# One of seven block products, P4, moved behind the last unit and taken in two levels

## The chip, the cores and the metric

The kernel runs on one core of a Trainium2 chip. Its time is device microseconds of that core, the median of a few runs. The engines are PE (TensorE: matmuls, with PEld its weight loads), DVE (VectorE), ACT (ScalarE), POOL (GpSimd, used here mostly to issue transfers) and SP (SyncE, which issues the loads of q, k and v).

## The reference

Everything is float32 here. A linear attention with decay is followed by a two-layer block:

```python
for b in range(nb):                       # blocks of 64 tokens
    intra = ((qb @ kb.T) * Dmask) @ vb    # Dmask = lam ** (i - j) below the diagonal
    inter = (qb * lam_pow) @ kv_state
    out = intra + inter
    kv_state = lam ** 64 * kv_state + (kb * rev_pow).T @ vb
x = out as (3072 tokens, 512)
h = x @ w_in                              # (512, 2048): the first product
g = h - tanh(h)
return g @ w_out                          # (2048, 512): the second product
```

## The kernel before, in words

The 3072 tokens go through in six groups (`NG`, g = 0 to 5) of 512 tokens: 128 positions of each of four sequences. Each group has an attention part, a first product and a second product; the attention of group g + 1 is woven into the products of group g.

**Strassen's seven products.** The 2048 columns of `w_in` are cut into four units u of 512. Within a unit weights and tokens are two by two blocks, and the product is taken as the Winograd form of Strassen's method: seven products P1 to P7 of half-sized blocks instead of eight. `FACT` (line 596) names the two factors of each; P4 is A22 (the second half of the unit's columns, the second half of the 512 inner rows) times T4 (a combination of tokens). The four results of a unit are `hidden(g, 11)`, `12`, `21` and `22` (in the trace all `g`), each 128 partitions by 512 columns per unit. P4 counts in 21 alone.

**Two levels.** In groups from the third on (`GI = 2`), P1 and P5 are cut once more: `inner_steps` (line 728) takes each as seven products of quarter blocks, each step for all four units at once, 4 matmuls of 128 columns. Its small weight combinations come from DRAM (`fine_in`), where `inner_weights` (line 706) writes them once, during the second group; its token combinations are made by `inner_tokens` (line 716). P2, P3, P4, P6 and P7 are one level: `up` (line 626) issues 4 matmuls of 256 columns for one unit. The second product is in two levels too: `down_twice` (line 915), seven steps of 4 matmuls of 128 columns.

**One unit** (`up`, lines 632 to 675). P1 and P5 have been added up in SBUF (`gS` and result 22). ACT seeds three PSUM banks from there (`seeded`, line 618): w, y and z. P2 adds to w, P6 and then P7 and P4 to y, P3 to z. Out of w comes 11; the state of y after P6 is copied into 12 (line 661), to which z is added (line 673); the state after P7 is added to 22 (line 664); y after P4 is 21. Each result r becomes r - tanh(r): tanh on ACT into a `th` tile (line 650, two buffers), the subtraction on DVE (line 655). Then two sums follow on DVE (`up_sums`, lines 697 and 698).

**The order.** `later_units` (line 1238) writes the order out. Unit 0: P2 of the next unit, P3, sums, P4. Units 1 and 2: P6, P2 of the next unit, P7, P3, sums, P4. Unit 3: P6, P3, P7, sums, the quarter sums for the second product's first part (`sums_twice(g, 4)`, three DVE operations of 512 columns), then the "cover", then P4. The cover is an attention block of the next group (`att_both`: lines 510, 496, 460, 524, ending in two copies by ACT into `xt`, line 414); in the sixth group it is product 1 of the second product (`down`, line 869). Then `later_products` starts with `down_twice(g, 4)`.

**What sets order and waits.** Operations marked `tied` or `hold` stay in program order on their engine; the others are placed by the tile framework's scheduler. Each engine runs its queue in order. Of the eight PSUM banks four are `ya`, `yb`, `w` and `z`, and four rotate under the tag `att`: the attention block takes two for its results and two for scores, and the two accumulators of `down_twice(g, 4)` take the next in turn, which are those two of the results that the xt copies read. The pieces of the second product's weights are loaded by POOL into a ring of 7 tiles, in the order of `pieces_of` (line 772): a load is issued when a tile of the ring comes free. Small sums of tokens, weights and quarters share one pool of four tiles (`sums`). In the third group DVE and POOL also make the fine weight combinations for two more parts (`fine_factors`, line 843: `made[g, 1]` and `made[g, 2]`, four adds each, given out along the units).

Of the kernel before, what the change touches and what calls it, by code (L numbers as in the profile page):

```python
# [24 lines left out]
def kernel(  # L25
# [116 lines left out]
    def tied(yes, op):  # L142
        return tc.keep_in_program_order(op) if yes else op
# [74 lines left out]

    fine_in = dram.tile([2, 3, 128, NU, 128], F32, name="fine_in")
    w_in_u = moe_w_in.rearrange("k (u a n) -> k u a n", u=NU, a=2)  # L220
# [405 lines left out]
    def up(g, u, n, wait=False, inside=False):  # L626
# [30 lines left out]
        if g >= GI:  # L657
            if n == 2:
                finish(11, t)
            elif n == 6:  # L660
                nc.scalar.activation(dst(12), t, AF.Copy)
            elif n == 7:
                def end():
                    tied(inside, nc.vector.tensor_tensor(dst(22), dst(22), t, op=AL.add))  # L664
                    finish(22, dst(22))

                if wait:
                    return end
                end()
            elif n == 4:  # L670
                finish(21, t)
            else:
                tied(inside, nc.vector.tensor_tensor(dst(12), dst(12), t, op=AL.add))  # L673
                finish(12, dst(12))
            return
# [23 lines left out]

    INNER = (1, 5)  # L700
    toks = {}

    def a_quarter(n, u, i, k):
        return w1[u][:, k, 0, ts(i, 128)] if n == 1 else ws[u][:, 0, k, ts(i, 128)]

# [9 lines left out]

    def inner_tokens(g):
        for n in INNER:
            x = xt[g][FACT[n][1]]
# [3 lines left out]
            for dst, x, y in ((t1, b12, b11), (t2, b22, t1), (b12, b22, b12), (t4, b21, t2)):  # L722
                nc.vector.tensor_tensor(dst, x, y, op=AL.subtract)
            toks[g, n] = {1: b11, 2: b21, 3: b22, 4: t4, 5: t1, 6: t2, 7: b12}

    STEPS = (1, 5, 2, 6, 7, 3, 4)

    def inner_steps(g, n, tag):
# [4 lines left out]
        for x in STEPS:  # L733
            b = toks[g, n][x]
            wb = piece(g, ("in", n), x) if x in (3, 5, 6) else None
            dst = w if x == 2 else z if x in (3, 5) else y
            for u in range(NU):
                a = wb.rearrange("p m c -> p (m c)")[:, ts(u, 128)] if wb is not None else a_quarter(
                    n, u, *{1: (0, 0), 2: (0, 1), 7: (1, 0), 4: (1, 1)}[x])
                tied(True, nc.tensor.matmul(out=dst[:, ts(u, 128)], lhsT=a, rhs=b, start=x in (1, 2, 5) and u == 0,  # L740
                                            stop=True, skip_group_check=True))
            d = dst.rearrange("q (u c) -> q u c", u=NU)
# [29 lines left out]
    def pieces_of(g):  # L772
        if g >= GI:
            yield from ((g, ("in", 5), x) for x in STEPS if x in (5, 6, 3))
        for n in order(g):
# [462 lines left out]
    def later_units(g):  # L1238
        for n in (1, 2):
            made[g, n] = fine_factors(n) if g == GI else iter(())  # L1240
        for u in range(NU):
            if u < 2:
                next(made[g, u + 1], None)
            for n in ("next", 3, "S", 4) if u == 0 else (6, "next", 7, 3, "S", 4) if u + 1 < NU else (
                    6, 3, 7, "S", "P4", "cover", 4):
                if n == "next":
                    up(g, u + 1, 2, inside=True)
                elif n == "S":
                    up_sums(g, u)
                elif n == "P4":  # L1250
                    sums_twice(g, 4)
                elif n == "cover":
                    if twice(g, 1):
# [6 lines left out]
            if u == 0:  # L1260
                every(made[g, 1])
            elif u == NU - 1:
                every(made[g, 2])

# [37 lines left out]
    for g in range(1, NG):  # L1302
# [6 lines left out]
        if g == NG - 1:  # L1309
            down_end(g)  # L1310
            continue
        inner_tokens(g + 1)
        p3 = down_twice(g, 3)
# [47 lines left out]
```

## Time and profile before

| | us |
|---|---|
| median of three runs (656.47 to 660.67) | 657.89 |
| the profiled execution | 657.6 |
| its span, first to last instruction | 655.8 |
| PE busy | 642.0 |
| DVE busy | 494.0 |
| ACT busy | 241.3 |
| POOL busy | 230.9 |
| mean granted PE clock | 0.997 of full speed |

A line of the timeline gives the start, the duration, the engine, the line of the kernel, the operation, the tile written and the tiles read, the shape and the count; in brackets the idle time of the engine before it and what ended it. One float32 matmul shows as two MATMUL records, so a step of 4 matmuls is "x8". The displayed duration of matmuls contains the end of the pipeline; the time that a step takes is from its start to the start of the next. A line of a stage gives the stretch, its length, the busy time of PE, PEld, DVE, ACT and POOL with the number of instructions, the granted clock, and the DMA engines' share and rate.

### The profile page before, as it was taken

To read this page: it belongs to the slowest core of one execution; us is meant where nothing else is said; L and a number is where in the kernel's file an instruction comes from. 1 tells how busy PE (TensorE), PEld (TensorE's weight loads), DVE (VectorE), ACT (ScalarE), POOL (GpSimd) and SP (SyncE) were. 2 spreads that over 40 slices of the span, in tenths; PEclk is the share of its full clock that TensorE was granted. 3 is DMA by queue.
4 is the path that set the end of the run, shared out by engine and by line. 5 is a ranking of instruction groups with operands and counts; after the bars stand their busy time and mean duration, and the time that the engine had idled before them with its cause. 6 is when DMAs were issued, how large, how long until landed. Compare 5 with 4: busy or idle time off the path is not lost.

```text
span 655.8 us, 14778 instructions
## 1 busy us (share of the span) xinstructions
PE 642.0 (98%) x5792; PEld 590.4 (90%) x5792; DVE 494.0 (75%) x884; ACT 241.3 (37%) x484; POOL 230.9 (35%) x396
## 2 busy tenths in 40 slices
PE   8899899999999999999999999999999999999998
PEld 6688688888888999989999988999988999988997
DVE  4688788896975986898868787878777888356583
ACT  3688565422321223443122453222354212444110
POOL 2120145775012545342556100546301356300450
PEclk9999999999999999999999999999999999999999
DMA  9979958999558877999878776779692487610582
GB/s 215 216 208 186 246 182 271 338 324 329 133 138 202 265 240 256 229 258 283 302 245 286 198 143 141 230 238 298 204 198 97 149 293 254 212 43 0 157 280 79
DMA packets 108261, 140.45 MB, mean 214 GB/s; under 512 B 64032, under 2 KB 81568, under 8 KB 108192
## 3 DMA queue, kind: packets, MB, share of 16 engines
q0 software_dynamic: 29840, 97.54, 46.5%
q1 hardware_dynamic: 78208, 41.96, 27.7%
q8 instruction: 46, 0.75, 0.5%
q14 instruction: 23, 0.19, 0.1%
q10 hardware_dynamic: 144, 0.00, 0.0%
HBM read 117.18 MB, written 23.86 MB: 215 GB/s over the span
## 4 chain that ended last, share of the span: by engine, by line
PE 75%; DVE 4%; DMA 3%; issue 1%; POOL 1%; ACT 1%; DVEq 0%; ACTq 0%; POOLq 0%
PE y L642 17%; PE y L934 16%; PE zw L934 12%; PE z L642 6%; PE w L642 5%; PE y L740 4%; PE z L740 2%; PE acc L1044 2%; PE y L869 2%; DMA wb<-fine 2%; PE sp L460 2%; PE op L510 1%; PE op L496 1%; PE w L740 1%; PE end L993 1%
## 5 line engine op out<-in xcount | busy, mean ns | idle before, releaser
L816 POOL DMA_DIRECT2D wb<-fine x217 | 116.7, 539 | 216.8 <-PE y L934 110.3
L934 PE MATMUL y<-wb,g 128*128 128x128 f32 x624 | 81.3, 276 | 0.5 <-DVE ss L467 0.4
L937 ACT ACTIVATE q<-y 128x128 f32<-128x128 f32 x108 | 29.9, 277 | 135.0 <-PE y L934 135.0
L934 PEld LDWEIGHTS y<-wb,g 128*128 128x128 f32 x624 | 75.3, 192 | 1.3 <-DVE ss L467 0.5
L934 PE MATMUL zw<-wb,g 128*128 128x128 f32 x416 | 55.2, 276 | 0.7 <-DMA wb<-fine 0.7
L934 PEld LDWEIGHTS zw<-wb,g 128*128 128x128 f32 x416 | 50.6, 192 | 1.1 <-DMA wb<-fine 1.1
L1014 PE MATMUL h<-xt,w 128*128 128x256 f32 x192 | 45.9, 393 | 1.1 <-DVE w L325 1.1
L642 PE MATMUL y<-xt,w 128*128 128x256 f32 x200 | 46.9, 380 | 0.0
L650 ACT ACTIVATE th<-g 128x512 f32<-128x512 f32 x42 | 26.5, 630 | 51.8 <-DVE g L673 19.7
L1014 PEld LDWEIGHTS h<-xt,w 128*128 128x128 f32 x192 | 36.8, 196 | 7.1 <-DVE w L325 1.0
L642 PEld LDWEIGHTS y<-xt,w 128*128 128x128 f32 x200 | 37.6, 190 | 5.1 <-ACT g L682 0.2
L655 DVE TENSOR_TENSOR g<-g,th 128x512 f32<-128x512 f32 x42 | 29.1, 692 | 17.4 <-ACT th L650 17.2
L642 PE MATMUL w<-xt,w 128*128 128x256 f32 x168 | 40.4, 382 | 0.0
L642 PE MATMUL z<-xt,ws 128*128 128x256 f32 x168 | 39.7, 379 | 0.0
L642 PE MATMUL y<-tt,w 128*128 128x256 f32 x160 | 38.1, 381 | 0.0
L642 PE MATMUL y<-tt,ws 128*128 128x256 f32 x160 | 38.1, 380 | 0.0
L642 PEld LDWEIGHTS z<-xt,ws 128*128 128x128 f32 x168 | 31.9, 190 | 4.3
L642 PEld LDWEIGHTS w<-xt,w 128*128 128x128 f32 x168 | 31.0, 190 | 4.5 <-ACT w L613 0.4
L642 PEld LDWEIGHTS y<-tt,w 128*128 128x128 f32 x160 | 30.1, 190 | 4.3 <-DVE g L664 0.2
L642 PEld LDWEIGHTS y<-tt,ws 128*128 128x128 f32 x160 | 30.0, 190 | 3.9
L934 PE MATMUL y<-wb,s 128*128 128x128 f32 x248 | 32.8, 275 | 0.1
L934 PE MATMUL zw<-wb,s 128*128 128x128 f32 x248 | 32.8, 275 | 0.0
(216 smaller groups left out, 1373.6 us busy)
## 6 DMA issues: line engine op xcount, KB each, us to landing
wb<-fine POOLq DMA_DIRECT2D x217, 256.0 KB, 3.8
fine<-f POOLq DMA_DIRECT2D x24, 256.0 KB, 5.3
wb<-fine_in POOLq DMA_DIRECT2D x24, 256.0 KB, 4.2
raw<-in_moe_w_out_dram POOLq DMA_DIRECT2D x10, 512.0 KB, 6.6
raw<-in_moe_w_in_dram SPq DMA_DIRECT2D x8, 512.0 KB, 5.2
raw<-in_moe_w_in_dram SPq DMA_DIRECT2D x16, 256.0 KB, 6.3
q_blk<-in_q_dram SPq DMA_DIRECT2D x32, 128.0 KB, 3.9
k_blk<-in_k_dram SPq DMA_DIRECT2D x32, 128.0 KB, 4.7
```

The costliest lines, as they stand in the source:

```text
L460: tied(True, nc.tensor.matmul(out=dst, lhsT=keys(p, j, late_), rhs=qt[ts(j, 64), p, rows], start=True, stop=True))
L496: tied(True, nc.tensor.matmul(out=dst(n, pp, j), lhsT=state[r, b, pp, :], rhs=tr[g, b][2][r, pp, :], start=not begun and n == 0 and p == 0 ...
L642: tied(g == 0, nc.tensor.matmul(out=t[:, m, :], lhsT=wt[:, kt, ts(m, 128)], rhs=x[:, kt, :], start=first and m == 0 and kt == 0, stop=kt = ...
L650: tied(g == 0, nc.scalar.activation(th, src, AF.Tanh))
L655: tied(g == 0 or g >= GI and inside, nc.vector.tensor_tensor(dst(c), src, th, op=AL.subtract))
L740: tied(True, nc.tensor.matmul(out=dst[:, ts(u, 128)], lhsT=a, rhs=b, start=x in (1, 2, 5) and u == 0, stop=True, skip_group_check=True))
L816: nc.gpsimd.dma_start(out=t.rearrange("p m c -> p (m c)"), in_=fine[TWICE.index(n_), SLOT.index(x_)].rearrange("p u c -> p (u c)"))
L869: nc.tensor.matmul(out=t[:, m, :], lhsT=a[:, u, kt, ts(m, 128)], rhs=wb[:, kt, :], start=first and u == 0 and m == 0 and kt == 0, stop=u = ...
L934: tied(True, nc.tensor.matmul(out=dst, lhsT=a[:, u, :], rhs=wb[:, ts(u, 128)], start=x in begins and u == 0, stop=u == NU - 1, skip_group_ ...
L937: nc.scalar.activation(keep, dst, AF.Copy)
L1014: tied(u == 0 or u == 2 and cs[0] == 11, nc.tensor.matmul(out=hm[c][:, m, :], lhsT=w1[u][:, i, a, ts(m, 128)], rhs=xt[0, t][:, i, :], star ...
L1044: nc.tensor.matmul(out=acc[n][:, r, :], lhsT=a[:, ts(r, 128)], rhs=b, start=kt == 0 and r == 0, stop=kt == KH - 1, skip_group_check=True)
```

## The change

From the third group on, P4 of the four units is no longer taken unit by unit. After P7 of each unit ACT copies the state of y into result 21. Behind unit 3's sums one new step, `inner_last`, takes P4 of all four units in two levels: seven sub-steps of 4 matmuls of 128 columns, in the banks ya, w, z and one of `att`. ACT copies three of its intermediate states, DVE adds four of them to the quarters of result 21. Behind the three quarter sums for the second product, `finish_last` adds the last intermediate state (one DVE operation of 1024 columns) and does the four tanh and the four subtractions of result 21. The cover then has no P4 behind it.

The small weight combinations of A22 are written during the second group beside those of P1 and P5 (4 DVE operations and one transfer more a unit); three more pieces a group are loaded through the ring. The token combinations of T4 are made by four small DVE operations: in the third group behind unit 3's sums and the last of the factor adds, later ahead of unit 3's P6. The last factor add moves from behind the last unit to behind unit 3's sums.

On ACT's queue the changed program has, at the end of the first product of the third to fifth group: the copy w, tanh of 22, the copy r5, the copy z, the probe of the attention block, the four tanh of result 21, the two xt copies. In the sixth group the four tanh stand before the copy of product 1.

```diff
-    INNER = (1, 5)
+    INNER = (1, 5, 4)
     def a_quarter(n, u, i, k):
-        return w1[u][:, k, 0, ts(i, 128)] if n == 1 else ws[u][:, 0, k, ts(i, 128)]
+        return (w1[u][:, k, 0] if n == 1 else ws[u][:, 0, k] if n == 5 else w1[u][:, 2 + k, 1])[:, ts(i, 128)]
...
             elif n == 7:
                 def end():
+                    nc.scalar.activation(dst(21), t, AF.Copy)
                     tied(inside, nc.vector.tensor_tensor(dst(22), dst(22), t, op=AL.add))
...
+    def inner_matmuls(g, n, x, dst, begin):
+        b = toks[g, n][x]
+        wb = piece(g, ("in", n), x) if x in (3, 5, 6) else None
+        for u in range(NU):
+            a = wb.rearrange("p m c -> p (m c)")[:, ts(u, 128)] if wb is not None else a_quarter(
+                n, u, *{1: (0, 0), 2: (0, 1), 7: (1, 0), 4: (1, 1)}[x])
+            tied(True, nc.tensor.matmul(out=dst[:, ts(u, 128)], lhsT=a, rhs=b, start=begin and u == 0,
+                                        stop=True, skip_group_check=True))
+
+    LAST = (1, 5, 6, 2, 7, 3, 4)
+
+    def inner_last(g):
+        y, w, z5, z3 = bank("y3", "ya", 1), bank("w3", "w", 1), bank("z5", "att", 4), bank("z3", "z", 1)
+        r5 = otile("r5")
+        out4 = hidden(g, 21)
+        c11, c12, c21, c22 = (out4[:, :, i, ts(j, 128)] for i in range(2) for j in range(2))
+        for x in LAST:
+            dst = {2: w, 3: z3, 5: z5}.get(x, y)
+            inner_matmuls(g, 4, x, dst, x in (1, 5))
+            if x in (1, 6):
+                nc.scalar.activation(w if x == 1 else z3, y, AF.Copy)
+            elif x == 5:
+                nc.scalar.activation(r5, z5, AF.Copy)
+            else:
+                c = {2: c11, 7: c22, 3: c12, 4: c21}[x]
+                hold(c, c, dst.rearrange("q (u c) -> q u c", u=NU), op=AL.add)
+        return r5
+
+    def finish_last(g, r5):
+        c = hidden(g, 21)
+        cols = c[:, :, :, ts(1, 128)]
+        hold(cols, cols, r5.rearrange("q (u c) -> q u c", u=NU)[:, :, None, :].to_broadcast([128, NU, 2, 128]), op=AL.add)
+        for u in range(NU):
+            th = work.tile([128, 2, HB], F32, name="th", tag="th")
+            nc.scalar.activation(th, c[:, u], AF.Tanh)
+            hold(c[:, u], c[:, u], th, op=AL.subtract)
...
-            yield from ((g, ("in", 5), x) for x in STEPS if x in (5, 6, 3))
+            yield from ((g, ("in", n), x) for n in (5, 4) for x in STEPS if x in (5, 6, 3))
...
-            for n in ("next", 3, "S", 4) if u == 0 else (6, "next", 7, 3, "S", 4) if u + 1 < NU else (
-                    6, 3, 7, "S", "P4", "cover", 4):
+            for n in ("next", 3, "S") if u == 0 else (6, "next", 7, 3, "S") if u + 1 < NU else (
+                    ("T",) * (g > GI) + (6, 3, 7, "S") + ("T",) * (g == GI) + ("U4", "P4", "cover")):
...
                 elif n == "S":
                     up_sums(g, u)
+                    if u + 1 == NU:
+                        every(made[g, 2])
+                elif n == "T":
+                    inner_tokens(g, (4,))
+                elif n == "U4":
+                    r5 = inner_last(g)
                 elif n == "P4":
                     sums_twice(g, 4)
+                    finish_last(g, r5)
...
             if u == 0:
                 every(made[g, 1])
-            elif u == NU - 1:
-                every(made[g, 2])
```

More of the change, by code (lines that the diff above doesn't have):

```diff
@@ L217 @@
     fine = dram.tile([len(TWICE), len(SUB), 128, NU, 128], F32, name="fine")
-    fine_in = dram.tile([2, 3, 128, NU, 128], F32, name="fine_in")
+    fine_in = dram.tile([3, 3, 128, NU, 128], F32, name="fine_in")
     w_in_u = moe_w_in.rearrange("k (u a n) -> k u a n", u=NU, a=2)
@@ L714, in inner_weights, with inner_tokens @@
             nc.gpsimd.dma_start(out=fine_in[INNER.index(n)].rearrange("x p u c -> p u x c")[:, u], in_=t[:, 0:3])
-    def inner_tokens(g):
-        for n in INNER:
+    def inner_tokens(g, ns):
+        for n in ns:
             x = xt[g][FACT[n][1]]
@@ L722, in inner_tokens @@
             for dst, x, y in ((t1, b12, b11), (t2, b22, t1), (b12, b22, b12), (t4, b21, t2)):
[L723 removed]
+                tied(n == 4, nc.vector.tensor_tensor(dst, x, y, op=AL.subtract))
             toks[g, n] = {1: b11, 2: b21, 3: b22, 4: t4, 5: t1, 6: t2, 7: b12}
     STEPS = (1, 5, 2, 6, 7, 3, 4)
+    def inner_matmuls(g, n, x, dst, begin):
[31 more added lines that the diff above has]
+            hold(c[:, u], c[:, u], th, op=AL.subtract)
     def inner_steps(g, n, tag):
@@ L733, in inner_steps @@
         for x in STEPS:
-            b = toks[g, n][x]
-            wb = piece(g, ("in", n), x) if x in (3, 5, 6) else None
             dst = w if x == 2 else z if x in (3, 5) else y
[L737 to L741, printed above, removed]
+            inner_matmuls(g, n, x, dst, x in (1, 2, 5))
             d = dst.rearrange("q (u c) -> q u c", u=NU)
@@ L1311 @@
             continue
-        inner_tokens(g + 1)
+        inner_tokens(g + 1, (1, 5))
         p3 = down_twice(g, 3)
```

## The prediction

> **What bounds the kernel now.** I read the page's totals first, then what the matmul engine (PE) waited for, then busy time by stage, then the timeline around the edited place in the fourth group (g = 3).
>
> ```profile
> PE 642.0 (98%) x5792; PEld 590.4 (90%) x5792; DVE 494.0 (75%) x884; ACT 241.3 (37%) x484; POOL 230.9 (35%) x396
> ```
>
> ```profile
> PE zw L934 <- DMA wb<-fine: 0.7, 2, 0.3
> PE sp L460 <- DVE kt L354: 0.5, 2, 0.3
> PE y L934 <- DVE ss L467: 0.4, 1, 0.4
> ```
>
> ```profile
> 272.00:307.00 35.00, 35.00 (x332) 30.88 (x333) 31.28 (x48) 15.66 (x29) 9.11 (x15) 1.00 1.09 275
> 376.00:411.00 35.00, 35.00 (x329) 31.00 (x326) 26.77 (x40) 15.71 (x29) 0.00 (x0) 1.00 0.69 140
> ```
>
> PE is the bound: 98% busy, and these three, its only listed waits from the second group on, come to 1.6 us in all (waited-for line, total, times, longest). The two stage rows (third and fourth group, first product; after the span the columns are PE, PEld, DVE, ACT, POOL) say more: PE is full, but DVE is at 31.3 and 26.8 of 35 us, so it has little room. Whatever shortens PE there meets DVE next.
>
> ```profile
> 395.77 1.89 PE L642 MATMUL z<-xt,ws 128*128 128x256 f32 x8
> ...
> 397.49 1.89 PE L642 MATMUL y<-tt,w 128*128 128x256 f32 x8
> ...
> 398.13 0.70 DVE L673 TENSOR_TENSOR g<-g,z 128x512 f32<-128x512 f32 x1
> ...
> 398.93 0.63 ACT L650 ACTIVATE th<-g 128x512 f32<-128x512 f32 x1 [1.55 <-DVE g L673]
> ...
> 399.22 1.89 PE L642 MATMUL y<-tt,ws 128*128 128x256 f32 x8
> 399.46 0.58 ACT L618 ACTIVATE z<-g 128x512 f32<-128x512 f32 x1
> ...
> 400.95 1.89 PE L642 MATMUL z<-xt,ws 128*128 128x256 f32 x8
> ...
> 404.49 1.15 PE L510 MATMUL op<-ss,v_nat 128*64 128x64 f32 x32
> ...
> 407.84 0.70 PE L524 MATMUL op<-ss,v_nat 64*64 64x64 f32 x32
> ...
> 408.46 1.99 PE L642 MATMUL y<-tt,w 128*128 128x256 f32 x8
> 408.52 1.08 ACT L414 ACTIVATE xt<-op 128x512 f32<-128x512 f32 x2 [1.60 <-PE op L524]
> ...
> 410.30 1.05 PE L934 MATMUL y<-wb,g 128*128 128x128 f32 x8
> 410.56 0.60 ACT L650 ACTIVATE th<-y 128x512 f32<-128x512 f32 x1 [0.95 <-PE y L642]
> ...
> 411.19 1.06 PE L934 MATMUL zw<-wb,g 128*128 128x128 f32 x8
> ```
>
> In order: P3 of unit 2, its P4, P6 and P3 of unit 3. P3 of unit 3 waits for the seed of bank z (399.46 to 400.04), which stands behind unit 2's add and tanh; P4 at 397.49 is part of what hides that. Below: the attention block (404.49 to 408.46), then P4 of unit 3, which hides the two copies xt (408.52 to 409.60) before the second product begins at 410.30. That product's two accumulators lie in the banks those copies empty. So P4 is cover at both places.
>
> **The change, part by part.**
> PE. A P4 step (4 matmuls of 256 columns) is 1.727 us from start to start (395.77 to 397.49); four make 6.91 a group. The new form is 7 steps of 4 matmuls of 128 columns, each 0.893 (410.30 to 411.19): 6.25. Gain 0.66 a group, 2.6 over four groups, if nothing waits.
>
> Second group: 16 more small DVE subtractions (0.28 long, 0.20 apart, 0.8 a unit) and 4 more writes of fine_in. DVE idles 0.7 to 1.2 in each unit's chain there, which covers 0.8. POOL gets one write ahead of the second product's pieces, 0.76 of issuing; the last piece is needed about 6 us later. Without that cover: up to 1. I take 0.
>
> Loads: three more pieces a group (256 KB, 4.2 us to landing) in the ring of 7; while they sit there, four of the next product's pieces are fetched early instead of seven. Each new piece still has about 6.2 us before use, and the waits below add to that. 0; bounds 0 and 0.35 a group (the longest such wait in the trace).
>
> Fourth group, walked on the trace's clock.
> (a) Unit loop: without three P4 steps P3 of unit 3 could start at 400.95 - 5.18 = 395.77. The z seed ends 4.27 after P3 of unit 2 starts (400.04 - 395.77); that part of DVE's order is unchanged. P3 of unit 3 now comes two steps (3.45) later instead of three, so it waits 4.27 + 0.1 - 3.45 = 0.9. The other seeds (w, y) and the copies out of y, one more on ACT per unit, come out 0.05 to 0.2 ahead of PE. P3 starts at 396.65, P7 at 398.4, the new step at 400.1.
> (b) The new step: DVE still owes the last unit's two adds, two subtractions and two sums when it begins, and is free for the new adds (0.68 each, as the P5 adds of L892) at 404.4. PE's last sub-step must wait for the second of its four adds to leave bank y: 0.35. The step ends at 406.7.
> (c) The attention block follows, 0.1 + 3.97, to 410.75; nothing of P4 is left behind it.
> (d) ACT's queue in the changed program holds the four new tanh ahead of the two xt copies. Each tanh waits for DVE: the last add (from 406.85, 0.6), three sums for the second product (0.7, 0.6, 0.6), then one add of 1024 columns (1.22, as L838), to 410.57. Then tanh 0.63, and, as the th tile has two buffers, the third and fourth wait for the first and second subtraction: starts 410.6, 411.15, 412.0, 412.7. The first xt copy runs 413.25 to 413.85, and the second product starts at 413.95. It started at 410.30: 3.65 lost, of which 3.2 is this wait.
> Queued behind it: on PE the whole second product; on DVE, after the fourth subtraction, that product's next sums, of which the first is due 1.8 after its start, when DVE has been free since 414.0. The end of (d) is the new bound: eight links of DVE and ACT, 7.2 us, against 4.07 of attention block. Bounds for one group: -0.66 (all hidden), +4.6 (every margin of 0.05 to 0.2 missed).
>
> The fifth group has the same order and work: 3.65.
>
> Third group: DVE also makes the fine factors (8 adds L892, 0.7 each). Four stand in one run from 280.9 to 283.8, as before, and DVE is then the bound: following its order at the trace's spacing (0.6 between independent instructions, 0.72 between dependent ones, 0.95 for a transpose, one subtraction of P4 taken out), the z seed of unit 3 ends at 294.75 (before 296.67). P3 starts at 294.85 instead of 292.07: 2.8. Here the token sums stand behind the last unit's sums and the last factor add: the first is ready at 303.5, while PE asks for it at 299.2: 4.4. On POOL the last factor's store now stands ahead of two pieces of the second product instead of behind them; they wait with it to 303.3 and are due from 316 on. The new step ends at 308.95, (d) as above, and the second product starts at 316.2 instead of 306.59: 9.6 lost. Against it, ten steps after 306.59 took 10.0 instead of 8.93, with waits for the masks and for pieces; DVE and POOL no longer lag there, so about 1.0 comes back. 8.6; bounds 5 and 11.
>
> Sixth group: no attention block, so the copies and (d) drop out. The z seed waits 0.8. The cover is product 1, which accumulates in the bank that the new step's last add must first empty: 0.95. Sub-step wait 0.3; gain 0.66. Sum 1.4; bounds -0.66 and 2.
>
> Sum: 8.6 + 3.65 + 3.65 + 1.4 = 17.3. The profiled execution took 657.6 (span 655.8, 1.8 around it), so 674.9; the median of the three runs is 0.3 above it: 675.2.
>
> **Rivals.**
> 1. The clock drops after the new waits. At the start of this trace, after idleness, 16 passes of 128 columns (L344) took 3.57 us until the next instruction began (1.58 to 5.15), 0.22 each; later 8 take 0.893, 0.11 each. The granted clock reads 1.00 there, which speaks against a throttle, and after the first 40 us no wait of PE passes 0.4, so the trace can't tell. If every wait over 3 us (one of 4.4, three of 3.2) restarted such a spell, each would cost 3.57 - 1.79 = 1.8: 7.2 in all, 682.4. [...]
> 2. The unit loop keeps up and only the end waits: no z wait, no wait for token sums. For it: the fourth group's DVE idled 7.3 us from 376.6 to 410.3. Against it: those gaps were mostly waits for tanh, part of the same chain. Then 3 x 3.2 + 0.95 - 4 x 0.66 - 1.0 = 6.9: 664.8.
> 3. Not slower: PE stays the bound everywhere and only its shorter work shows, 657.9 - 2.6 = 655.3. Its place is (d): the first xt copy would have to end within the 4.07 us of attention block, in each of three groups. The chain there has 7.2; it decides when four of its links are gone or ahead.
>
> **How the numbers follow.** The walked waits 0.72, rival 1 0.12, rival 2 0.11, rival 3 0.03, anything else 0.02. The prediction is the likeliest, 675.2. Range 668.5 to 682.5: below, the third group at its lower bound (-3.6) with the small margins of the other groups better than walked (-3); above, rival 1. A measurement of this kernel tells about 1% (6.6 us) from no change. Slower by more than that: the walked case, rival 1, half of rival 2 and part of the rest, 0.90. Within 1%: the other half and some, 0.07. Faster: 0.03.
>
> **What would show it.** (a) A PE wait before P3 of unit 3, near 0.9 in groups four to six and 2.8 in the third, put down to ACT's seed. (b) In the third group alone, a wait of some 4 us in the new step, for DVE's token sums. (c, d) In groups three to five the first matmul of the second product idle for about 3.2, released by ACT's xt copy, with four tanh just ahead of it. (e) The sixth group's product 1 idle about 1 behind DVE's last add. (f) New sub-steps 0.89 apart. If the xt copies run before the tanh, or the second product starts right behind the attention block, (d) is wrong and most of the loss with it. If 0.22 passes follow the waits, rival 1 holds.

## The result, and the profile after

| | before | after |
|---|---|---|
| median, us (six runs each, taken together) | 655.28 (652.29 to 660.67) | 685.25 (682.53 to 688.91) |
| ratio | | 1.0464, 95% interval 1.0433 to 1.0496 |
| the profiled execution's span | 655.8 | 683.4 |

The change costs 30 us. The prediction was 675.2 with a range of 668.5 to 682.5: the sign and the places were right, the size was not, and the result lies outside the range.

The page of the changed kernel, its totals and its clock row:

```profile
PE 649.6 (95%) x5888; PEld 598.1 (88%) x5888; DVE 515.1 (75%) x936; ACT 255.2 (37%) x512; POOL 240.3 (35%) x412
...
PEclk9999999999999999988999999999999999999999
```

PE now does less arithmetic but is busy for 7.6 us longer, and the granted clock, 9 in every slice before, falls to 8 in two slices, both in the third group. What PE waited for (total, times, longest):

```profile
PE y L967 <- ACT xt L414: 9.1, 3, 3.1
PE z L642 <- ACT z L618: 5.8, 4, 2.1
PE z L735 <- DVE tt L724: 4.2, 1, 4.2
PE zw L967 <- DVE g L925: 1.6, 1, 1.6
...
PE zw L967 <- DVE gS L925: 1.0, 1, 1.0
PE y L902 <- DVE g L925: 0.8, 1, 0.8
```

All four waits of the prediction are there, at its places: the xt copies, the z seed, the token sums, product 1's bank. The two of `zw` for DVE are not in the prediction; they lie in the second group. Now the stages that the prediction showed, first product of the third and of the fourth group (span, then PE, PEld, DVE, ACT, POOL busy, granted clock, DMA share, GB/s):

```profile
271.34:317.76 46.42, 37.04 (x325) 32.83 (x321) 36.34 (x57) 17.88 (x33) 10.91 (x18) 0.92 0.95 240
389.06:427.68 38.62, 33.83 (x324) 29.90 (x321) 31.09 (x49) 17.64 (x33) 1.61 (x3) 1.00 0.63 142
```

In the two rows of before that the prediction shows, PE was busy without a gap; now it idles 9.4 and 4.8 us, and in the third group the clock is 0.92 besides.

To place the loss I cut each trace at the first step of every group that writes bank w from xt (`w<-xt`, read off PE's timeline). Us per stage, with the kernels that matter below:

| kernel | up to the second group | second | third | fourth | fifth | sixth, end | sum from the second on |
|---|---|---|---|---|---|---|---|
| before | 150.5 | 99.2 | 103.7 | 103.0 | 102.0 | 97.5 | 505.4 |
| after | 145.3 | 102.7 | 117.7 | 107.8 | 109.4 | 100.4 | 538.0 |
| predicted loss | 0 | 0 | 8.6 | 3.65 | 3.65 | 1.4 | 17.3 |
| measured loss | | 3.5 | 14.0 | 4.8 | 7.4 | 2.9 | 32.6 |

(The stage up to the second group has the same work in both kernels and took 144.5 to 152.3 in the 19 traces of this study, before or changed; it is left out of the sums. The medians, which include it, differ by 30.0.)

The fourth group's timeline, at the lines that answer to those shown of before:

```profile
405.31 1.89 PE L642 MATMUL z<-xt,ws 128*128 128x256 f32 x8
...
406.14 0.69 DVE L665 TENSOR_TENSOR g<-g,y 128x512 f32<-128x512 f32 x1 [0.86 <-ACT g L664]
406.75 1.11 DVE L354 STREAM_TRANSPOSE kt<-k_blk 128x512 f32<-128x512 f32 x1
...
408.30 0.67 DVE L674 TENSOR_TENSOR g<-g,z 128x512 f32<-128x512 f32 x1
...
409.60 0.58 ACT L618 ACTIVATE z<-g 128x512 f32<-128x512 f32 x1
...
410.24 1.99 PE L642 MATMUL z<-xt,ws 128*128 128x256 f32 x8 [1.31 <-ACT z L618]
...
423.21 1.22 DVE L925 TENSOR_TENSOR g<-g,r 128x1024 f32<-128x1024 f32 x1
...
424.52 1.15 ACT L764 ACTIVATE th<-g 128x512 f32<-128x512 f32 x2 [1.53 <-DVE g L925]
...
425.91 1.23 ACT L764 ACTIVATE th<-g 128x512 f32<-128x512 f32 x2 [0.24 <-DVE g L925]
427.05 1.07 ACT L414 ACTIVATE xt<-op 128x512 f32<-128x512 f32 x2
427.68 1.16 PE L967 MATMUL y<-wb,g 128*128 128x128 f32 x8 [3.12 <-ACT xt L414]
```

Step (d) of the prediction, link by link: the addition of 1024 columns, four tanh, the xt copies, the second product, 3.12 us late (3.2 predicted). The z wait is 1.31 instead of 0.9. Here no slow step follows: the product's next step begins 1.00 later. It is otherwise in the third group (PE's timeline):

```profile
292.67 3.42 PE L642 MATMUL z<-xt,ws 128*128 128x256 f32 x8 [2.07 <-ACT z L618]
295.88 2.20 PE L642 MATMUL y<-xt,w 128*128 128x256 f32 x8
297.91 1.05 PE L735 MATMUL y<-tt,w 128*128 128x128 f32 x8
303.15 1.96 PE L735 MATMUL z<-tt,wb 128*128 128x128 f32 x8 [4.19 <-DVE tt L724]
304.90 1.91 PE L735 MATMUL y<-tt,wb 128*128 128x128 f32 x8
306.61 1.12 PE L735 MATMUL w<-tt,w 128*128 128x128 f32 x8
...
317.76 2.08 PE L967 MATMUL y<-wb,g 128*128 128x128 f32 x8 [3.12 <-ACT xt L414]
319.63 1.92 PE L967 MATMUL zw<-wb,g 128*128 128x128 f32 x8
321.34 1.06 PE L967 MATMUL y<-wb,s 128*128 128x128 f32 x4
```

From start to start, P3 takes 3.21 where 1.73 is usual, the sub-step behind the 4.19 us wait 1.75 where 0.893 is, and the second product's first ones 1.87 and 1.71. These are matmuls at half rate. Added up over the steps behind the three waits, they cost 1.8 + 1.7 + 3.0 = 6.5 us in this group, and 1.7 behind the fifth group's 2.86 us wait: 8.2 us. The trace's own clock records say the same: the granted clock was 0.50 from 293.08 to 296.49, 303.32 to 306.73, 316.97 to 323.80 and 535.42 to 538.84, and up to 682 us nowhere else. PE was busy for 16.2 of these 17.1 us, which at half rate costs 8.1.

### The profile page after: what moved, and what is told of

Same layout as the page of the kernel before. It is cut to its first block, busy times and chain, and to the rows that moved or that the text cites. A ratio compares the mean times of both kernels' runs of the same rounds, so it can differ in the third digit from the quotient of the medians.

```text
span 683.4 us, 15057 instructions
## 1 busy us (share of the span) xinstructions
PE 649.6 (95%) x5888; PEld 598.1 (88%) x5888; DVE 515.1 (75%) x936; ACT 255.2 (37%) x512; POOL 240.3 (35%) x412
## 4 chain that ended last, share of the span: by engine, by line
PE 51%; issue 12%; DVE 8%; DMA 7%; POOL 4%; ACT 3%; SPq 1%; POOLq 0%; DVEq 0%; ACTq 0%
PE y L967 15%; PE zw L967 11%; PE y L735 6%; PE y L642 5%; PE z L735 3%; PE w L642 3%; PE z L642 2%; POOL wb L849 2%; DMA fine<-f 2%; PE w L735 1%; DVE g L655 1%; DVE g L925 1%; DMA out_dram<-q 1%; DMA fine<-wt 1%; PE y L902 1%
## 5 line engine op out<-in xcount | busy, mean ns | idle before, releaser
L967 PE MATMUL y<-wb,g 128*128 128x128 f32 x624 | 83.3, 280 | 9.2 <-ACT xt L414 9.1
L967 PE MATMUL zw<-wb,g 128*128 128x128 f32 x416 | 56.6, 280 | 1.6 <-DVE g L925 1.6
L967 PEld LDWEIGHTS zw<-wb,g 128*128 128x128 f32 x416 | 52.3, 197 | 1.8 <-DVE g L925 1.8
L642 PE MATMUL z<-xt,ws 128*128 128x256 f32 x168 | 41.6, 392 | 6.0 <-ACT z L618 5.8
L1047 PE MATMUL h<-xt,w 128*128 128x256 f32 x192 | 44.2, 382 | 1.0 <-DVE w L325 1.0
L655 DVE TENSOR_TENSOR g<-g,th 128x512 f32<-128x512 f32 x42 | 29.0, 691 | 17.1 <-ACT th L650 16.8
L925 DVE TENSOR_TENSOR g<-g,s 128x512 f32<-128x512 f32 x26 | 17.9, 689 | 21.6 <-PE zw L967 21.5
L967 PEld LDWEIGHTS y<-wb,s 128*128 128x128 f32 x248 | 31.0, 197 | 0.0
```

Source lines behind the costliest of these rows:

```text
L642: tied(g == 0, nc.tensor.matmul(out=t[:, m, :], lhsT=wt[:, kt, ts(m, 128)], rhs=x[:, kt, :], start=first and m == 0 and kt == 0, stop=kt = ...
L655: tied(g == 0 or g >= GI and inside, nc.vector.tensor_tensor(dst(c), src, th, op=AL.subtract))
L925: tc.keep_in_program_order(nc.vector.tensor_tensor(*args, **kw))
L967: tied(True, nc.tensor.matmul(out=dst, lhsT=a[:, u, :], rhs=wb[:, ts(u, 128)], start=x in begins and u == 0, stop=u == NU - 1, skip_group_ ...
L1047: tied(u == 0 or u == 2 and cs[0] == 11, nc.tensor.matmul(out=hm[c][:, m, :], lhsT=w1[u][:, i, a, ts(m, 128)], rhs=xt[0, t][:, i, :], star ...
```

## The experiments

Two theories stood after the comparison. **A**: three separate things add up, namely the waits as walked, half-rate matmuls behind PE's idle time, and something in the second group. **B**: DVE is the bound of the whole stretch, and a wait taken away at one place returns at another.

The added writes of g1 and g2 are overwritten by the products, and nobody reads the fillers of e10 and f2. The kernels with the cover ahead (e5, e6, e8, e9, f3, f4) compute a different A12 factor (result 21, as the second product uses it) than the reference; number, size and order of their instructions are as told, so they serve for the time alone.

### Idle time and the half rate: g1, g2, e10, f2

g1 and g2 are the kernel before, with waits put in. In `down_twice`:

```diff
+        for _k in range({2: 2, 3: 4, 4: 6, 5: 6}.get(g, 0) if n == 4 else 0):
+            nc.scalar.activation(y, hidden(g, 21 if g == NG - 1 else 11)[:, NU - 1]..., AF.Copy)
         y = y[:, 384:512]
```

> The kernel before with a wait put in on purpose: ahead of the second product's first matmul ScalarE writes that product's bank 2, 4 and 6 times in the third to fifth groups (behind the xt copies) and 6 times in the sixth (behind the last tanh of P4); the products write over it. By 0.53 us for each write and what lies ahead of it, TensorE waits about 1.7, 2.8, 3.9 and 5 us, 13.4 us in all. Theory A (TensorE runs at half rate after a wait of 2 us or more, for about 3 us): 655.3 + 13.4 + 3 x 1.5 to 3 x 1.8 = 673 to 674 us, with granted clocks of 0.8 in the slices behind the waits. [...] Rival C (the slow steps of the changed kernel do not come from its waits): every step 0.893 us from the first on, 668.7 us.

Measured: 673.47 us, ratio 1.0274 (1.0226 to 1.0322). The waits came out as 0.38, 1.81, 3.28 and 5.27 us, 10.7 in all. Only the last was followed by slow steps, of 2.4 us. That speaks against A, which had expected three spells; four cases settle little. Hence g2, with twelve waits in the same manner.

> The kernel before with twelve waits put in, to see how long a wait must be: ScalarE writes the first bank of the second product's products 4, 7 and 5 ahead of their first matmul, 7 times (4 in the sixth group), 3 times and 5 times, in the third to sixth groups. By g1 (0.38, 1.81 and 3.28 us for 2, 4 and 6 writes) the waits are about 4, 2 and 3 us, some 36 us in all. Theory A (a wait of 2 us or more is followed by half-rate steps): twelve spells of 1.5 to 3 us, 655.3 + 36 + 18 to 36 = 709 to 727 us. [...] Theory A'' (by chance of where the wait falls: those of 4 us always, of 3 us about every second, of 2 us now and then): 6 to 8 spells, 698 to 710 us.

Measured: 719.43 us (two runs), ratio 1.097 (1.0887 to 1.1052). Two of its twelve waits, from PE's timeline:

```profile
318.34 1.16 PE L939 MATMUL y<-wb,g 128*128 128x128 f32 x8 [2.26 <-ACT y L925]
319.34 1.63 PE L939 MATMUL zw<-wb,g 128*128 128x128 f32 x8
320.76 1.92 PE L939 MATMUL y<-wb,s 128*128 128x128 f32 x8
...
425.29 1.95 PE L939 MATMUL y<-wb,g 128*128 128x128 f32 x8 [3.81 <-ACT y L925]
427.04 1.92 PE L939 MATMUL zw<-wb,g 128*128 128x128 f32 x8
```

Every one of the twelve (2.26 to 4.53 us, 41.4 in all) is followed by slow steps, 1.4 to 3.1 us each, 24.6 in all. 41.4 + 24.6 = 66.0; the stages from the second group on grew by 67.2. So idle PE time costs a second time in this kernel, also in a program without the change. C is out. The mean granted clock of this run is 0.962, against 0.997 in the profile of before. Twelve spells and the time are what A forecast, but g1's wait of 3.28 us had none, so A's rule of 2 us isn't it either; A'' fits in kind, though its number of spells was too low. What the traces of before and after show of it stands in the last section. Note the first case: the slow steps begin one step after the wait, at 319.34, not at once (1.00 us from start to start for the step before, 1.42 for this one).

e10 and f2 are the reverse: the changed kernel, with PE kept busy in the four waits by matmuls into a bank that nobody reads.

```diff
+            if x == 5 and g == GI:
+                warm(18)                      # f2: 9
             inner_matmuls(g, 4, x, dst, x in (1, 5))
...
+        if n == 4 and GI <= g < NG - 1:
+            warm(13)                          # f2: 6
```

> The changed kernel with its longest waits filled by matmuls whose result nobody reads: 18 of 128x256 (3.9 us by 1.73 us for 8) ahead of the fifth quarter product's step in the third group, where TensorE waits 4.19 us, and 13 (2.8 us) ahead of the second product's first step in the third to fifth groups, where it waits 3.12, 3.12 and 2.86. Nothing else is moved: each stage starts when it did. Theory A (the half-rate steps come from TensorE's own idle time): the steps behind these places take 0.893 us from the first on; the 1.7, 3.0 and 1.6 us go: 685.2 - 6 = 679 us. Rival C (they come from something else, such as the load of the whole chip at that time): the slow steps stay, and the filling itself may run at half rate and overrun its wait by up to 3.9 us: 685 to 693 us.

Measured: 693.06 us, ratio 1.0569 (1.0506 to 1.0633). The size was my mistake: I had counted the 8 records of a line as 8 matmuls, where they are 4, so the fillers ran 7.9 and 5.7 us and overran the waits by some 12 us in all. By the time alone this is a miss. The steps behind them, though, are all at full rate: 0.89 from the first one on, at all four places, and the mean granted clock of the profiled run is 0.995, against 0.987 in after. f2 has half as many.

> As e10, with half the filling: 9 and 6 matmuls of 128x256, which by e10's trace (18 in 7.87 us, 13 in 5.72 us) take 3.9 and 2.6 us, so that they end inside the waits of 4.19 and 3.12 us. Theory A (TensorE's idle time makes the half-rate steps): no slow step behind these four places, each stage starts when it did: 685.2 less the 1.7, 3.0 and 1.6 us of the changed kernel's trace, 679 us, and 680.5 where the slow steps behind the wait for the seed of z stay as they are. Rival C: the slow steps come all the same, 685 us.

Measured: 686.29 us, ratio 1.0449 (1.0398 to 1.0501): no gain, against 679 to 680.5. PE's timeline in the third group:

```profile
301.50 4.15 PE L743 MATMUL warm<-w 128*128 128x256 f32 x18 [0.52 <-DVE g L665]
305.48 1.05 PE L735 MATMUL z<-tt,wb 128*128 128x128 f32 x8
306.38 1.06 PE L735 MATMUL y<-tt,wb 128*128 128x128 f32 x8
...
318.97 0.34 PE L524 MATMUL op<-ss,v_nat 64*64 64x64 f32 x5 [3.74 <-issue]
```

Behind the filler the sub-steps again start 0.89 apart, as theory A says, and the fifth group is 2.3 us shorter than after (107.1 against 109.4). But in the third PE stood still for 3.74 us in the attention block, released by nothing that the profile shows ("issue"), and the second group was 0.9 longer. Such waits without a releaser, of 0.2 to 3.7 us, stand in nine other traces of changed kernels, and in none of after, e2, e3, e7, e10 and f1. What held PE there no run shows. So the rate is shown by the steps; the time of f2 doesn't show it.

### The three waits: e1, e2, e3, e7, e4

e1 moves the end of result 21 into the steps of the next product, and ties tanh and result copies in that order:

```diff
                     sums_twice(g, 4)
-                    finish_last(g, r5)
+                    late_fin[g] = finish_last(g, r5)     # now yields after each unit
...
         product = down_twice(g, 4)
-        steps(product, 4)
+        for _ in range(4):
+            next(product)
+            next(late_fin[g])
```

> The changed kernel with the end of the A12 factor (the addition of r5, four tanh and four subtractions) moved from ahead of the xt copies into the steps of the next product, two tanh behind the first result copy and two behind the second. Theory A (the walk: the four tanh stand ahead of the two xt copies in ScalarE's order, and each wait in the third and the sixth-but-one groups is followed by half-rate matmuls): the waits of the second product's first matmul for the xt copies, 3.12 + 3.12 + 2.86 = 9.1 us, go, and with them the slow steps behind two of them (about 3.0 us in the third group and 1.6 us in the fifth): 685.2 - 13.7 = 671.5 us. Theory A without the clock (the slow steps come from something else, not from these waits): 685.2 - 9.1 = 676. Rival B (the product cannot begin earlier anyway, since VectorE's sums for it or its weight pieces are late too): the wait is there under another name, 682 to 686 us.

Measured: 676.47 us, ratio 1.0345 (1.0291 to 1.0398); 8.8 us below after. The waits for xt fell from 9.1 to 2.0 (0.69, 0.69, 0.68), the result copies behind the tanh add 1.1. So 6.0 us of waits went, and with them the slow steps behind them: the mean granted clock is 0.995 over 674.0 us, what two stretches of 3.41 us at 0.50 make; in after the waits for z and for the token sums, which e1 leaves, have one each behind them. The mechanism is theory A's; of the 5.0 us by which its 671.5 was missed, the 3.1 us of waits that stayed are the greater part. B's "another name" came to those 1.1 us at most.

e2 makes the third group's token sums ahead of unit 3, in a tile of the result pool:

```diff
-                    ("T",) * (g > GI) + (6, 3, 7, "S") + ("T",) * (g == GI) + ("U4", "P4", "cover")):
+                    ("T", 6, 3, 7, "S", "U4", "P4", "cover")):
```

> The changed kernel with the token sums of the third group made before the last unit's three products, as in the later groups, in a tile of their own. Theory A: the 4.19 us wait of the fifth quarter product for VectorE's token sums goes, and with it the slow steps right behind it (1.75, 1.71 and 0.95 us where 0.893 is usual, 1.7 us in all): 685.2 - 5.9 = 679.3 us; if the slow steps stay, 681. Rival B (VectorE has too much to do in that stretch, with the factor sums of the outer weights): the four sums ahead of the last unit push its additions back, and the wait of the last unit's P3 for the seed of z grows by as much: 684 to 686 us.

Measured: 681.89 us, ratio 1.041 (1.0365 to 1.0456); 3.4 us below. The third group falls from 117.7 to 108.4. The 4.19 us wait is gone; 0.6 came back at the last sub-step. Its 3.13 us xt wait had no slow steps this time. But the fourth is 1.9 longer than after, with slow steps behind an xt wait that had none there: which wait is followed by them differs from run to run.

e3 only exchanges 3 and 7 in that tuple.

> The changed kernel with the last unit's products in the order P6, P7, P3 instead of P6, P3, P7, so that P7 stands over the time in which the seed of z is written. Theory A: the four waits for the seed (2.07, 1.31, 1.31 and 1.15 = 5.8 us) go, with the slow steps behind the one of the third group (1.5 us for the P3 and 0.5 for the next); the token sums of the third group come 0.5 us later at most: 685.2 - 7.3 = 678 us. Rival B (what follows the units waits for P3's end instead: the bank of z is read by the small product's sixth step, and the sums of the next product need P3's factor): about 1 us is given back in each group, 681 to 684 us.

Measured: 690.82 us, ratio 1.0536 (1.0495 to 1.0577); 5.6 us above after. The scheduler still set half of P3 ahead of P7, so the z waits stayed at 5.8; the token sums' wait rose to 5.35, and the fourth to sixth groups got a wait of 0.8 each for DVE in the last sub-step. As a test of the order it failed; it shows only that this half-exchange hurts. e7 takes the other way to the z seed: only the transposes (406.75 in the timeline above) go one place earlier.

```diff
-                          for n, (u, c) in enumerate(((0, 12), (1, 22), (1, 12), (2, 22)))})
+                          for n, (u, c) in enumerate(((0, 22), (0, 12), (1, 22), (1, 12)))})
```

> The changed kernel with only the four block transposes of VectorE moved: the one between the third unit's P7 and P3 goes to the first unit. Theory A (the last unit's P3 waits because the addition that frees the bank of z stands behind a 1.1 us transpose on VectorE): the waits of 1.31, 1.31 and 1.15 us fall to 0.2 to 0.3 us, the third group's 2.07 us by about 1.1, together some 4 us, and 1.5 us of slow steps may go with the latter: 685.2 - 4 = 681 us, down to 679.5. Rival B (the chain P3, addition, tanh, seed is as long without it): 684 to 686 us.

Measured: 690.97 us, ratio 1.0521 (1.047 to 1.0572); 5.7 us above after. Its waits:

```profile
...
PE z L735 <- DVE tt L724: 6.2, 1, 6.2
PE y L735 <- DVE g L925: 3.9, 2, 2.0
PE y L642 <- ACT g L661: 3.1, 5, 0.7
...
PE z L642 <- ACT z L618: 1.2, 1, 1.2
```

The z wait fell from 5.8 to 1.2, more than theory A asked for. But the token sums now come 6.2 late, the last sub-step waits 3.9 for DVE's adds, and the copies out of y 3.1. The time that PE won, it lost further down, where DVE had not become any faster. For the z wait theory B holds: it is DVE's lag, shown at one place or another.

e4 is e1, e2 and e3 together.

> The three edits together: tanh behind the xt copies, token sums ahead, P7 before P3. Theory A: the waits 9.1 + 4.2 + 5.8 = 19.1 us go and the half-rate steps behind them (about 8 us in all) with them: 685.2 - 27 = 658 us, so within 1 per cent of the kernel before, above it by the wait of the sixth group's product 1 (0.8 us), the small waits inside the units and what is still late. Rival B (the waits are one backlog on VectorE that shows at one place or another): 664 us or more. A gain over the kernel before (below 654 us) would need all the 0.66 us of matmul time in each of four groups and no new wait.

Measured: 677.58 us, ratio 1.0336 (1.0299 to 1.0374): no better than e1 alone. 3.8 us of waits for DVE in the last sub-steps came in, of the kind that e3 has. A's sum of 658 fell, and the time lies where B put it, "664 or more". Which of the three edits brings that in, e4 alone can't tell; f5 below leaves e3 out.

### The cover ahead: e8, e9

e8 puts the attention block ahead of the small P4, whose four partial results then stand in the attention's banks; tanh as in e1. Earlier forms of e8 and e9, with the banks in another order (e5 and e6), took 673.31 and 670.56 us, where theory A had given about 669 and 661.

```diff
+                    ("P4", "cover", "U4") if g < NG - 1 else ("U4", "P4", "cover"))):
```

> The cover ahead of the small P4 once more, with the small P4's four banks in another order: the two partial sums that start with a copy stand in the banks of the attention's outputs, which are written over all 512 columns, so that nothing of them is lost (in e5 and e6 a quarter of their columns was written over). Theory A: as in e5, whose fast span was about 672 us with 3.4 us of waits for weight pieces and 1.8 us for the masks' sums: 670 to 674 us; the small P4's first step no longer waits for the xt copies. Rival B: the first result bank of the small P4 is drained last and is now the second bank of the next product, whose second step waits 0.5 to 1 us in each of three groups: 672 to 676 us.

Measured: 671.33 us, ratio 1.0229 (1.0175 to 1.0283), within theory A's 670 to 674. There is no wait for xt or token sums; in their place come 0.9 for the masks' sums in two groups and 0.3 to 1.0 for weight pieces. Its sixth group, too, is as short as before, 97.6 us: there the order is that of after, and only the banks and the place of the four tanh differ. e9 adds the order P6, P7, P3, now tied on PE, and e7's transposes:

> As e8, with P6, P7, P3 held in that order on TensorE and the four transposes earlier. Theory A: as e6, 670 us or a little below, 3 us below e8. Rival B (the waits are one backlog on VectorE that shows at whichever place is next): no nearer to the kernel before than e8, 672 to 676 us.

Measured: 671.91 us, ratio 1.0249 (1.02 to 1.0298). The z waits are gone, and nothing is won: 3.0 us of waits for copies out of y and 1.8 for a seed of y stand in their place (0.7 and none in e8). This is B again, for z.

### The second group: f1, and all together

DVE's timeline of after in the second group, then f1's, at the first sums for the second product:

```profile
208.47 0.69 DVE L925 TENSOR_TENSOR s<-g 128x512 f32<-128x512 f32 x1
212.39 0.69 DVE L925 TENSOR_TENSOR s<-s,g 128x512 f32<-128x512 f32 x1 [3.24 <-DMA fine_in<-ws]
```

```profile
212.93 0.69 DVE L926 TENSOR_TENSOR s<-g 128x512 f32<-128x512 f32 x1
213.65 0.69 DVE L926 TENSOR_TENSOR s<-s,g 128x512 f32<-128x512 f32 x1
```

In after the second sum waits 3.24 us for a transfer that it has nothing to do with: the write of weight sums, which still holds one of the four tiles that all DVE sums share. PE then waits 1.60 and 1.00. f1 gives the last unit's sums for A22 another tile:

```diff
-            t = late["pool"].tile([128, 4, 128], F32, name="ws2", tag="sums", bufs=4)
+            t = (otile("ws4").rearrange("q (x c) -> q x c", x=4) if (u, n) == (NU - 1, 4)
+                 else late["pool"].tile([128, 4, 128], F32, name="ws2", tag="sums", bufs=4))
```

> The changed kernel with one tile moved: the weight sums for A22 of the second group's last unit are made in a tile of the result pool instead of one of the four that VectorE's other sums share. Theory A (in the second group VectorE's second sum for the next product waits 3.24 us for a tile that the write of the weight sums still holds, and TensorE then waits 1.60 and 1.00 us): that wait falls back to the 0.91 us of the kernel before, TensorE's two waits go, and the second group is 2.6 to 3.1 us shorter: 685.2 - 3 = 682.3 us, with the second group's first to last marker at 62.3 to 62.8 us instead of 65.4. Rival B (it is the writes themselves, behind one another on one queue, whatever the tile): the wait moves to the next user of a tile, 685 us.

Measured: 684.08 us, ratio 1.0415 (1.0366 to 1.0465). The medians, 1.2 us apart, can't tell it from after. The stage can: the second group takes 99.8 us, against 102.6 to 104.1 in the twelve changed kernels that share the tile and 99.6 in the three others that don't (f3, f4, f5). Both of PE's waits there are gone. That part of A is shown.

f3 and f4 are e9 and e8 with f1's tile and the sixth group's small P4 in its old banks.

> All together: the cover ahead of the small P4, tanh in the next product, P6, P7, P3 in that order, transposes earlier, the weight tile of f1, and the sixth group's small P4 in its old banks. From e9's 671.9 us: less 3 us by f1, plus 0.8 us for the sixth group's bank: 669.7 us. Faster than the kernel before only if the rest (waits of 0.3 to 0.9 us at some fifteen places) were gone too; not expected.

> As f3 with the last unit's order P6, P3, P7 and the transposes left where they are, so with the waits for the seed of z. From e8's 671.3 us: less 3 us by f1, plus 0.8 us: 669.1 us. If the waits for z (5.8 us) are worth their length, f4 is some 5 us above f3; if they only show VectorE's backlog, it is level with f3.

Measured: f3 669.68 us, ratio 1.0211 (1.0166 to 1.0256); f4 672.25, ratio 1.0239 (1.0184 to 1.0294). 2.6 us apart, inside their intervals, with z waits in one and none in the other: level rather than 5 apart. The old banks cost the sixth group more than the 0.8 us expected: 100.9 and 100.2 us, against 97.6 to 97.8 in e5, e6, e8 and e9, whose small P4 stands in the attention's banks there too. With tanh moved but the old banks it is 100.5 (e1). So the 2.9 us that the change loses in the sixth group lie almost wholly with the choice of banks: neither z nor product 1 waits there in e8, 1.15 and 0.78 us in f4.

f5 takes the three causes out (e1, e2 and f1) and leaves the rest as it is.

> The changed kernel with the edits of e1 (tanh in the next product), e2 (token sums of the third group ahead) and f1 (tile of the weight sums) together. Theory A (three separate causes that add up): by stages of the traces, from e1's 674.0 us of span: third group 112.9 to about 106.5 (the 4.19 us wait and 1.9 us of slow steps go, 0.6 us of e2's new wait comes), second group 103.1 to 99.8: 664.4 us with e1's first stage of 145.2 us, about 667 us with a middling one, and a median near 668; the waits for the seed of z stay. Rival B (one backlog on VectorE): the wait taken from the token sums comes back in the same group, as in e4, whose third group is about 5 us longer than that: 672 us or more.

Measured: 672.89 us, ratio 1.0264 (1.0226 to 1.0302). The second group is 99.6, fourth and fifth are 106.8 and 105.7, as in e1. The third is 111.9 instead of 106.5, and its timeline shows what is left:

```profile
290.72 2.84 PE L642 MATMUL z<-xt,ws 128*128 128x256 f32 x8 [2.04 <-ACT z L618]
302.20 1.16 PE L737 MATMUL y<-tt,w 128*128 128x128 f32 x8 [0.29 <-DVE g L928]
...
311.42 0.72 PE L970 MATMUL zw<-wb,g 128*128 128x128 f32 x5 [1.96 <-issue]
```

By the time alone this is B's forecast, "672 us or more". Its mechanism, though, isn't there: the token sums don't come back under another name (0.29). Of the 5.4 us too much in the third group 3.7 are the 1.96 us without a releaser and a stretch at clock 0.50 behind it (1.7); the rest is not placed. None of the versions comes nearer to the kernel before than 2%, by their medians.

## Why the prediction was right or wrong

**Right: the waits.** The walk of DVE's, ACT's and PE's order gave the places, the releasers and nearly the lengths. (b) 4.4 predicted, 4.19 measured. (c, d) 3.2 in three groups: 3.12, 3.12, 2.86, with the four tanh ahead of the copies, as e1 shows by moving them. (e) 0.95: 0.78. (a) 2.8, 0.9, 0.9, 0.8: 2.07, 1.31, 1.31, 1.15. In the last three groups (a) is 0.4 short. It took DVE's part of the chain as unchanged. The order is, the block transpose (406.75 above) stood there before too; but the add behind P7 (406.14) now waits 0.86 for ACT's new copy of the state of y, and the add that frees z starts 2.99 us after unit 2's P3 instead of 2.36.

**Wrong: the clock, the step that failed most.** I priced half-rate matmuls as rival 1, at 0.12, and took 0 for the sum, on two grounds. Neither holds. The granted clock of 1.00 at the start of the trace is no reading: its clock records begin only at 7.1 us, and a stretch without records counts as 1.00. And "after the first 40 us no wait of PE passes 0.4, so the trace can't tell" misread the trace of before. At 75 us PE waits 2.63 us for a load of k, and the 16 records of L1014 behind it take 5.30 instead of 3.62, at a clock of 0.50 (the row gives the stretch, PE busy, the clock, DMA share and GB/s):

```profile
71.07 3.62 PE L1014 MATMUL h<-xt,w 128*128 128x256 f32 x16
...
77.75 0.41 PE L376 MATMUL tp<-ident,k_nat 128*128 128x128 f32 x2 [2.63 <-DMA k_nat<-in_k_dram]
...
78.59 5.30 PE L1014 MATMUL h<-xt,w 128*128 128x256 f32 x16
```

```profile
78.78:82.19 3.41, 3.41 (x9) 0.50 0.26 67
```

So rival 1 holds in kind, and the trace could tell. Its price was 7.2, the trace of after has 8.2. That these are so near is in part luck, since the waits that pay are others than the four I named: the third group's xt and token waits and the fifth's xt wait did, the fourth's 3.12 us did not, and the 2.07 us wait for z did, which I hadn't counted.

**Wrong: the second group.** "I take 0", with up to 1 for POOL, was 3.5. I had counted DVE's 0.8 us a unit and POOL's issue, but not the tile: one more write holds one of four shared tiles, and DVE's next sums wait for it. f1 takes it back. The trace of before has such a wait already:

```profile
217.51 0.69 DVE L892 TENSOR_TENSOR s<-gS 128x512 f32<-128x512 f32 x1 [0.91 <-DMA fine_in<-ws]
```

**Too small: the small waits.** Fourth group 3.65 predicted, 4.8 measured: z 1.31, a copy out of y 0.34, xt 3.12, the sub-steps 0.53 longer than 7 x 0.893, less 0.66, make 4.6. I had counted on 0.05 to 0.2 of spare time ahead of the copies. The fifth is the same plus 1.7 of slow steps and some 0.9 in gaps of 0.1 to 0.4; the sixth 2.9 instead of 1.4, z 1.15, product 1 0.78 and the same small gaps.

Summed: 17.3 predicted, 8.2 for the half rate, 3.5 for the second group, 3.6 for the rest (fourth 1.15, fifth 2.05, sixth 1.5, and -1.1 in the third, whose waits were shorter than walked) make 32.6, what the stages show. Of that the 8.2 rest on g2, e10 and the clock records, the 3.5 on f1, and the sixth group's 2.9 on the comparison of e8 with f4; the other small waits are read from the trace alone.

## What to carry to other kernels

A step that looks like plain arithmetic on the bounding engine may be the cover of two chains on others; walk those chains with the cover gone, link by link, as here, where most waits came out to a few tenths (4.19 for 4.4, 3.12 for 3.2 us). Then price each wait of PE twice, once for its length and once, with a chance, for matmuls at half rate behind it: in after they cost 1.8 us behind the wait of 2.07, 1.7 behind 4.19, 3.0 behind the third group's 3.12, 1.7 behind 2.86, and nothing behind the fourth group's 3.12. And with every added write ask which buffer it holds until it has landed, and who is next in line for that buffer.

## What the runs showed of the hardware

In the traces of before and after the granted clock is 1.00 or 0.50 in every record. The first record begins 7.10 and 6.36 us into the span; from there on each record that ends inside the span lasts 3.41 us or a whole multiple of it (after: 286.72, 3.41, 6.83, 3.41, 10.24, 6.83, 211.63, 3.41 and 143.36 us; before: 71.68, 3.41 and 573.44). Those at 0.50 last 3.41 us, four times, or 6.83, once. I took PE's busy time in each stretch of 3.41 us, counted from the first record, that itself had a clock of 1.00 and has a whole one behind it:

| PE busy in the stretch, us | stretches, before and after | followed by one at 0.50 |
|---|---|---|
| 0.17 to 1.35 | 5 | 5 |
| 1.78 or more | 375 | 0 |

The five are 0.84 us in before, with the wait for k (75.36 to 78.78), and 1.35, 0.17, 1.08 and 0.64 us in after, with the waits for z, for the token sums and for xt in the third and the fifth group. The two 3.12 us waits of after, in the third and the fourth group, fall on different sides:

```profile
313.56:316.97 3.41, 1.08 (x64) 1.00 0.00 0
316.97:320.38 3.41, 2.62 (x12) 0.50 0.02 5
422.78:426.20 3.42, 1.78 (x96) 1.00 0.03 5
426.20:429.61 3.41, 1.93 (x17) 1.00 0.00 0
429.61:433.02 3.41, 3.41 (x33) 1.00 0.68 192
```

The third group's wait (314.64 to 317.76) lies in one stretch but for its end, and PE is busy for 1.08 of 3.41 us there: half rate follows, for two stretches. The fourth group's (424.56 to 427.68) is divided at 426.20, with 1.78 and 1.93 us busy on its two sides: nothing follows. The two waits are of one length; what differs between them is how much falls into one stretch. Between 1.35 and 1.78 us busy neither trace has a stretch, and where the limit lies, or whether other kernels have the same, was not shown. One stretch of 3.41 us at 0.50, with PE busy throughout, costs half of it by an estimate from its length and clock, 1.71 us; the three sub-steps behind the 4.19 us wait took 1.75, 1.71 and 0.95 us where 0.893 is usual, 1.7 us more.
